# The second matrix of a channel MLP as seven products of quarters, with weights through DRAM and a new instruction order

## The chip, the core and the metric

The kernel runs on one core of one Trainium2 chip. The metric is the device time of one execution in microseconds; the median of several runs is what is compared. The engines are TensorE (PE in the profile; PEld is its weight load), VectorE (DVE), ScalarE (ACT), GpSimd (POOL) and SyncE (SP), which issues every DMA of this kernel.

## What is computed

Three blocks in a chain, on a batch of 4, a sequence of 576 and a width of 512, in float32:

```
# 1 block-causal attention, 8 heads of 64, blocks of 64 positions
scores = q @ k.T / 8, masked where block(i) < block(j);  x = softmax(scores) @ v
# 2 channel mixing with the token before
xk, xr = lerp(x, x_prev, mu_k), lerp(x, x_prev, mu_r)
x = sigmoid(xr @ w_r) * (relu(xk @ w_k)**2 @ w_v)          # 512->512, 512->1024->512
# 3 MLP mixer
u = x + (relu(x.T @ w_tok1) @ w_tok2).T                    # over tokens, 576->256->576
out = u + relu(u @ w_ch1) @ w_ch2                          # over channels, 512->1536->512
```

The change is about the last product, `relu(u @ w_ch1) @ w_ch2`: 2304 tokens, 1536 hidden channels, 512 outputs.

## The kernel before, in words

**Precision.** TensorE takes float32 operands in a rounded form (`F32R`). To keep accuracy every operand is split into a high part (the rounded value) and a low part (the rest), and each product is three matmuls: high by high, high by low, low by high (`mm3`, line 941; `mm_high` and `mm_low`, lines 928 and 933, for channel mixing). The splitting is work for the other engines: a cast for the high part (`copy`, line 467, on ScalarE or VectorE) and a subtraction for the low part (`less`, line 470, on VectorE or GpSimd). Weights come in as 64-bit floats and are first joined into one word (`split_chunk`, lines 485 to 522: steps `load`, `top`, `join`, `high`, `low`).

**Stages.** Attention (`attention`, `unit`, `pv`): for each batch element, each pair of heads and each block of 128 queries, scores (line 670), a mask (a memset of PSUM, line 698), the largest value (line 704), exponentials (line 723), the normalised probabilities as two float16 parts (lines 474, 476 and 750), a DMA transpose (line 756) and the product with v (line 835). Channel mixing (`channel_mix`): lerp and split (`mix`: steps `shifted`, `here`, `high`, `low`), then 240 matmuls of 256 or 320 columns for each part of a batch element; its result goes to DRAM (`xd`, line 1040) and comes back as `x` (line 1061). Token mixing (`front`, four of them). Channel MLP (`back`, five token tiles: one of 256 columns, four of 512): `split` and `rest` make the operand, twelve `g_group` steps of 12 matmuls make the hidden layer in PSUM (banks `b`), `g_high` (line 1178, ScalarE) and `g_low` (line 1181, VectorE) write its two parts, sixteen `y_group` steps of 9 matmuls make the four output blocks, `y_out` (line 1193) adds `u`, and `store` (line 1196) writes the result. The two parts of `w_ch2` are converted into SBUF once, in `c2a` (after channel mixing ends) and `c2b` (after the fronts end), and stay there.

**Order.** Every piece of work is a step with an engine, dependences and buffers (`Plan.step`). `Plan.schedule` plays all steps through with a table of costs (`c_pe`, `c_v`, `c_a`, `c_g`, `LAND` for a DMA's landing, a shared port for GpSimd and some VectorE steps) and emits the instructions of all engines in the order in which this play starts them; on each engine they then run in that order. Two long tables written into the file steer it: `RANK`, the priority of each of the 3464 steps (a permutation), and `ON`, the engine of each step that may run on more than one. `FILL` lets the plan put small matmuls of no use (line 538) into TensorE's planned gaps between two times of the plan.

Of the kernel before, what the change touches and what calls it, by code (L numbers as in the profile page):

```python
# [31 lines left out]
N2 = 3 * NC1 // 4  # L32
# [8 lines left out]
          "shifted", "square", "one"}  # L41

FILL = (4.0, 90.0)
FIFO = ("xh", "xl", "l", "o", "xt0", "xt1", "qkh", "uh")
CS, CV = 410, 256
LX, LPE, LSE, LAND = 0.15, 0.2, 0.12, 2.31
# [4 lines left out]
    xt0=4, xt1=4, mt=4, xh=8, xl=8, r=4, bxh=2, bxl=2, h1h=2, h1l=2, uh=4,  # L51
)

RANK = [int(x) for x in """
# [192 lines left out]
def c_v(n, psum=False):  # L247
    return 0.067 + n / 960 + 0.06 * psum


def c_v2(n):
    return 0.067 + n / 1920


def c_a(n, psum=False, ap=False):
    return (0.053 if psum else 0.093) + n / 1200 + 0.09 * ap
# [26 lines left out]
class Plan:  # L283
# [58 lines left out]
    def schedule(self):  # L342
# [21 lines left out]
        while done < len(self.steps):  # L364
# [39 lines left out]
            if s.shared:  # L404
                t = max(t, port)
                port = t + cost
# [1085 lines left out]
```

## Time and profile before

| | us |
|---|---|
| median of 3 runs (lowest, highest) | 792.9 (792.04, 796.18) |
| the profiled execution's own time | 793.54 |
| span of its profile | 791.8 |
| busy in the span: PE, PEld | 770.0, 673.3 |
| busy in the span: DVE, ACT, POOL | 499.9, 374.3, 116.7 |

The busy time of an engine is the union of its instructions' spans. A matmul's end is modelled and includes the way through the array, so a busy TensorE says that something was in flight, not that matmuls followed at the full rate; the rate is read from the distance of starts.

### The profile page before, as it was taken

What the parts mean: (1) busy time and instruction counts of PE and PEld (TensorE: products, weight loads), DVE (VectorE), ACT (ScalarE), POOL (GpSimd) and SP (SyncE); (2) the same over time, 40 slices, a digit from 0 to 9 for tenths busy, and PEclk for the clock granted to TensorE, in tenths of its full rate; (3) what the DMA queues carried; (4) which work ended last, traced back from release to release, by engine and by line L of the source; (5) the groups of instructions that cost most, each with busy time, mean ns of one, the idle gap of its engine ahead of it and who ended that gap; (6) DMA issues with size and microseconds to landing.
All of it is one profiled execution on the core that took longest, in us unless ns stands there. A gap on an engine that the chain in (4) does not pass through costs nothing.

```text
span 791.8 us, 16348 instructions
## 1 busy us (share of the span) xinstructions
PE 770.0 (97%) x6315; PEld 673.3 (85%) x6315; DVE 499.9 (63%) x1311; ACT 374.3 (47%) x1010; POOL 116.7 (15%) x143
## 2 busy tenths in 40 slices
PE   7899999998999999999999999999999999999998
PEld 5678898888988899999999988988888888888886
DVE  8999999978999899887836889622112121302111
ACT  6999877678687576745433344212102111300110
POOL 1222231231022121423203112200000000000000
PEclk9999999999999999999999999999999999999999
DMA  8789974967757857566123664100010000001001
GB/s 289 266 201 191 176 159 96 182 117 128 164 106 141 174 123 142 89 135 230 41 79 107 192 231 144 53 28 1 0 41 1 13 27 15 14 1 54 0 1 53
DMA packets 130671, 83.26 MB, mean 105 GB/s; under 512 B 104353, under 2 KB 112161, under 8 KB 130081
## 3 DMA queue, kind: packets, MB, share of 16 engines
q1 hardware_dynamic: 130592, 82.22, 43.5%
q8 instruction: 49, 0.80, 0.4%
q14 instruction: 30, 0.24, 0.1%
HBM read 48.11 MB, written 9.44 MB: 73 GB/s over the span
## 4 chain that ended last, share of the span: by engine, by line
PE 67%; DVE 9%; DMA 4%; ACT 2%; issue 1%; ACTq 0%; DVEq 0%; SPq 0%
PE b L941 38%; PE l L928 11%; PE l L933 6%; PE b L1090 4%; PE b L1111 3%; DMA pt<-pin 3%; DVE pin L750 2%; PE s L670 2%; PE o L835 2%; DVE nm L704 1%; PE b L1066 1%; DVE mt L906 1%; ACT p L723 1%; DVE xl L470 0%; DVE r L1035 0%
## 5 line engine op out<-in xcount | busy, mean ns | idle before, releaser
L941 PE MATMUL b<-uh,wx 128*128 128x512 f32 (+1 forms) x480 | 142.5, 373 | 0.0
L1178 ACT ACTIVATE wy<-b 128x512 fp32r<-128x512 f32 (+1 forms) x60 | 33.0, 555 | 219.3 <-PE b L941 219.1
L928 PE MATMUL l<-xh,wx 128*128 128x256 f32 (+1 forms) x768 | 124.4, 302 | 1.8 <-DVE r L1035 1.5
L928 PEld LDWEIGHTS l<-xh,wx 128*128 128x128 f32 x768 | 108.4, 190 | 8.5 <-DVE r L1035 1.7
L941 PE MATMUL b<-wy,c2a 128*128 128x512 f32 (+1 forms) x460 | 111.3, 368 | 0.0
L941 PEld LDWEIGHTS b<-uh,wx 128*128 128x128 f32 x480 | 87.6, 189 | 17.4 <-issue 0.5
L941 PEld LDWEIGHTS b<-wy,c2a 128*128 128x128 f32 x460 | 79.5, 189 | 15.3
L928 PE MATMUL l<-kh,wy 128*128 128x256 f32 (+1 forms) x512 | 76.6, 299 | 0.3 <-DVE r L1035 0.2
L941 PE MATMUL b<-gx,wx 128*128 128x512 f32 x192 | 75.4, 393 | 0.0
L928 PEld LDWEIGHTS l<-kh,wy 128*128 128x128 f32 x512 | 70.3, 189 | 3.2 <-issue 1.2
L723 ACT ACTIVATE p<-s,nb 128x384 f32<-128x384 f32 (+4 forms) x120 | 67.4, 564 | 11.3 <-DVE nb L476 5.2
L1193 DVE TENSOR_TENSOR x<-b,x 128x256 f32<-128x256 f32 (+7 forms) x32 | 13.5, 455 | 93.5 <-PE b L941 93.5
L750 DVE SCALAR_TENSOR_TENSOR pin<-p,rs,pin 128x384 f16<-128x384 f32 (+3 forms) x104 | 67.4, 657 | 5.0 <-ACT pin L474 4.5
L933 PE MATMUL l<-xl,wx 128*128 128x320 f32 (+1 forms) x384 | 67.0, 300 | 0.0
L1181 DVE SCALAR_TENSOR_TENSOR gx<-b,wy 128x512 fp32r<-128x512 f32 x32 | 21.8, 690 | 67.7 <-ACT wy L1178 67.7
L704 DVE TENSOR_REDUCE nm<-s 128x2 f32<-128x256 f32 (+4 forms) x80 | 63.2, 796 | 0.7 <-PE s L670 0.2
L933 PEld LDWEIGHTS l<-xl,wx 128*128 128x128 f32 x384 | 56.4, 190 | 0.5
L474 ACT ACTIVATE pin<-p,rs 128x512 f16<-128x512 f32 (+3 forms) x78 | 48.9, 638 | 15.2 <-DVE rs L742 6.8
L835 PEld LDWEIGHTS <-vb 128*64 128x64 f16 x1824 | 45.2, 111 | 12.6 <-issue 10.1
L835 PE MATMUL o<-pt,vb 128*64 128x128 f16 (+1 forms) x1824 | 50.6, 212 | 5.3 <-DMA pt<-pin 5.2
L1181 DVE SCALAR_TENSOR_TENSOR wy<-b,wy 128x512 fp32r<-128x512 f32 (+1 forms) x28 | 16.1, 576 | 48.8 <-ACT wy L1178 48.7
L941 PEld LDWEIGHTS b<-gx,wx 128*128 128x128 f32 x192 | 36.1, 188 | 8.3
(146 smaller groups left out, 1389.3 us busy)
## 6 DMA issues: line engine op xcount, KB each, us to landing
wst<-in_w_c SPq DMA_DIRECT2D x24, 256.0 KB, 3.0
qkf<-in_kq SPq DMA_DIRECT2D x12, 480.0 KB, 4.7
v<-in_v SPq DMA_DIRECT2D x16, 320.0 KB, 3.4
x<-xd SPq DMA_DIRECT2D x4, 1152.0 KB, 8.1
wst<-in_w_c2a SPq DMA_DIRECT2D x18, 256.0 KB, 2.8
qkl<-in_w_v SPq DMA_DIRECT2D x16, 256.0 KB, 3.2
stage<-in_w_k SPq DMA_DIRECT2D x9, 410.0 KB, 4.4
qkf<-in_kq SPq DMA_DIRECT2D x12, 256.0 KB, 3.3
```

What stands on the lines that cost most here:

```text
L474: self.nc.scalar.activation(out=out, in_=x, func=AF.Copy, scale=by)
L704: nc.vector.tensor_reduce(out=c["nm"][:, :nh], in_=m, axis=AX.XY if j == 4 else AX.X, op=ALU.max, negate=True)
L723: nc.scalar.activation(out=c[x], in_=s, func=AF.Exp, scale=0.125, bias=c["nb"][:, x:x + 1], accum_out=c["sm"][:, x:x + 1],)
L750: nc.vector.scalar_tensor_tensor(out=like(pin[:, w:w + n]), in0=c[x], scalar=rs, in1=like(pin[:, :n]), op0=ALU.mult, op1=ALU.subtract)
L835: nc.tensor.matmul(o[hh * D:hh * D + D, q0:q0 + rows], v[:, i, y, hh, :], st["pt", hh, j][:, x * (j + 1) + i, :], start=i == x == y == 0, ...
L928: self.nc.tensor.matmul(ps, ww[:, k, :], x[0][k], start=k == 0 and n == 0, stop=False)
L933: self.nc.tensor.matmul(ps, w[0][:, k, :], x[1][k], start=False, stop=k == kt - 1)
L941: self.nc.tensor.matmul(ps, ww[k], xx[k], start=k == 0 and n == 0, stop=k == kt - 1 and n == 2)
L1090: nc.tensor.matmul(ps, ww[:k, i, m * P:(m + 1) * P], xx[:k], start=i == 0 and n == 0, stop=i == NJ - 1 and ww is self.w1[1],)
L1111: nc.tensor.matmul(ps[:, :HT], c[hh, m][:, i * P:(i + 1) * P], ww[:, m, sl], start=n == 0, stop=n == 5)
L1178: nc.scalar.activation(out=gh(m), in_=d["g", m][:, :n], func=AF.Relu)
L1181: nc.vector.scalar_tensor_tensor(out=gl(m), in0=d["g", m][:, :n], scalar=0.0, in1=raw(gh(m)), op0=ALU.max, op1=ALU.subtract)
```

## The change

The hidden layer's values `B` (1536 by 512 tokens of a tile) and the weights `A` (`w_ch2`) are cut into quarters: 768 hidden channels by 256 outputs of the weights, 768 hidden channels by 256 tokens of the hidden layer. In place of eight products of quarters the kernel makes seven, of sums and differences of quarters (Strassen's form, Winograd's order of sums):

- `load_c2` replaces `c2a` and `c2b`. Twelve times it loads two chunks of `w_ch2` (the same `load`, `top`, `join`, `high`, `low` as before), makes four sums of 128x128 blocks (`term`), splits them (`high`, `low` of 512 columns), and stores 1 MB to a new DRAM buffer `wd` (8 matrices of 12 KB per partition). It may start when attention is over, and must be done before the second half of the memory is laid out (`to_back`).
- `back`: `g_out` writes the hidden layer once, unsplit, in float32 (ScalarE or VectorE), in place of `g_high` and `g_low`. `operand` splits a quarter in three steps of `high` and three of `low`, 512 columns each; `term` makes a difference of quarters in three steps of 512 columns. A tile of 512 tokens has 7 operands and 4 terms. Four operand buffers are shared by all tiles (`op`).
- `product` fetches one matrix of `wd` (128 rows of 12 KB, 1.57 MB) into one of three buffers (`rg`) and issues 36 matmuls of 256 columns (line for line the pattern of `mm3`). `add`, `keep` and `join` bring the seven results to `u`, by 256 tokens and two output blocks at a time. A tile of 512 tokens has 252 matmuls of 256 columns in place of 144 of 512. The tile of 256 tokens has no Strassen form: four products, 144 matmuls of 256 columns as before.
- TensorE's other work is unchanged. `mask` may now run on ScalarE too (an activation that writes -8e9), memsets of the start may run on GpSimd, one early activation (`word`) loads the exponential's table, `FILL` reaches to 320 instead of 90, all buffer kinds but seven are now handed out in order of rank (`FIFO`), and the plan's costs differ a little.
- `RANK` and `ON` are new, for 3791 steps. Counted over the two `ON` tables, steps that are in both kernels changed engine as follows (V VectorE, A ScalarE, G GpSimd; the count before, then after):

```
attention: mask V 64->27, A 0->37;  bias V 39->25, A 41->55;  first part of p V 36->28, A 92->100;  low of q,k V 15->11, G 9->13
weights of stage 2: low V 24->15, G 7->16;  high V 12->10, A 19->21;  top V 4->10, A 27->21
mixing: shifted V 23->13, A 41->51;  high V 22->13, A 42->51;  low V 36->24, G 28->40
        hidden high V 27->22, A 37->42;  hidden low V 38->34, G 26->30;  square V 11->17, A 34->36, G 19->11
new in load_c2: term V 26, G 22;  high V 5, A 7;  low V 7, G 5 (of 512 columns)
new in back: g_out V 27, A 33;  operand high V 52, A 49 and low V 47, G 54;  term V 27, G 21;  add, join, keep V 52, G 11, A 3
```

The diff, cut to its core (both tables left out):

```diff
-N2 = 3 * NC1 // 4
+NH, HC = NC1 // 2, NC // 2
...
-FILL = (4.0, 90.0)
-FIFO = ("xh", "xl", "l", "o", "xt0", "xt1", "qkh", "uh")
+FILL = (4.0, 320.0)
-LX, LPE, LSE, LAND = 0.15, 0.2, 0.12, 2.31
+LX, LPE, LSE, LAND, LTURN, LAP = 0.15, 0.2, 0.12, 1.4, 0.9, 0.15
...
+FIFO = frozenset(BUFS) - {"v32", "vm", "vd", "ve", "vs", "tw", "wst"}
...
-            step("V", 0.14, mask, r=[ts], w=[ts])
+            step("any", both(0.2, 0.14), mask, r=[ts, "none"], w=[ts])
...
+    def operand(self, src, toks, gate):
+        o = Buf("op")
+        for i in range(3):
+            def high(e, i=i):
+                self.copy(e, self.ops[o.slot][:, 0, 2 * i:2 * i + 2], src(i))
+            def low(e, i=i):
+                t = self.ops[o.slot]
+                self.less(e, t[:, 1, 2 * i:2 * i + 2], src(i), raw(t[:, 0, 2 * i:2 * i + 2]))
+            self.step("any", both(c_a(NC), c_v2(NC)), high, r=toks(i) + gate, w=[(o, (i, 0))])
+            self.step("any", both(v=c_v(NC), g=c_g(NC)), low, r=toks(i) + [(o, (i, 0))], w=[(o, (i, 1))])
+        return o
+    def product(self, w, o, x, begin=True, end=True, turn=False):
+        r = Buf("rg")
+        def fetch():
+            self.nc.sync.dma_start(raw(self.rg[r.slot]), self.wd[:, w])
+        def product(fs, ks, first, last):
+            ps, a, t = self.xb[x.slot], self.rg[r.slot].rearrange("p (k f h m) -> p k f h m", k=NH, f=2, h=2), self.ops[o.slot]
+            n = 0
+            for k in ks:
+                for f in fs:
+                    for y, z in ((0, 0), (0, 1), (1, 0)):
+                        n += 1
+                        self.nc.tensor.matmul(
+                            ps[:, f * HC:(f + 1) * HC], a[:, k, f, y], t[:, z, k],
+                            start=first and n == 1, stop=last and n == 6 * len(ks) * len(fs) // 2,
+                        )
+        self.step("S", 0.55, fetch, r=["wd", "sw3"], w=[r], dma=NH * 4 * P / 704)
...
-        def g_high(m):
-            nc.scalar.activation(out=gh(m), in_=d["g", m][:, :n], func=AF.Relu)
-        def g_low(m):
-            nc.vector.scalar_tensor_tensor(
-                out=gl(m), in0=d["g", m][:, :n], scalar=0.0, in1=raw(gh(m)), op0=ALU.max, op1=ALU.subtract
-            )
-        def y_group(i, k0, k1):
-            if k0 == 0:
-                d["y", i] = self.ps_b.tile([P, 512], F32, tag="b", name="b")
-            g = [[f(m) for m in range(NC1)] for f in (gh, gl)]
-            self.mm3(d["y", i][:, :n], self.c2[i], g, NC1, k0, k1)
+        def g_out(m, e):
+            g = self.g[:, m // NH, m % NH, :n]
+            if e == "A":
+                nc.scalar.activation(out=g, in_=d["g", m][:, :n], func=AF.Relu)
+            else:
+                nc.vector.tensor_scalar(out=g, in0=d["g", m][:, :n], scalar1=0.0, scalar2=None, op0=ALU.max)
...
+        o_b11 = self.operand(b11, k11, gate)
+        self.term(sub, tx, b12, b11, two(k12, k11), kx)
+        o_t1 = self.operand(tx, kx, gate)
+        o_b21 = self.operand(b21, k21, gate)
+        o_b22 = self.operand(b22, k22, gate)
+        self.term(sub, tx, b22, tx, two(k22, kx), kx)
+        o_t2 = self.operand(tx, kx, gate)
+        self.term(sub, b22, b22, b12, two(k22, k12), k22)
+        o_t3 = self.operand(b22, k22, gate)
+        self.term(sub, b21, b21, tx, two(k21, kx), k21)
+        o_t4 = self.operand(b21, k21, gate)
+        self.product(0, o_b11, p[0])
+        keep(p[0], ts)
+        add(p[0], 0, 0)
+        self.product(4, o_t1, p[1])
+        add(p[1], 0, 1)
+        add(p[1], 1, 1)
+        self.product(1, o_b21, p[2])
+        add(p[2], 0, 0, final=True)
+        self.product(7, o_b22, p[3])
+        add(p[3], 0, 1)
+        self.product(5, o_t2, p[4])
+        join(p[4], ts)
+        add(ts, 0, 1, final=True)
+        self.product(6, o_t3, p[5])
+        join(p[5], ts)
+        add(ts, 1, 1, final=True)
+        add(ts, 1, 0)
+        self.product(3, o_t4, p[6], turn=c == 4)
+        add(p[6], 1, 0, parts=((0,), (1,)) if c == 4 else ((0, 1),), final=True)
+    def load_c2(self, stage):
...
-        conv("c2a", lambda: self.c2a, N2 * DM, DM, self.i["w_c2a"], ["sw2"])
-        conv("c2b", lambda: self.c2b, (NC1 - N2) * DM, DM, self.i["w_c2b"], ["sw3"])
+        self.load_c2(stage)
+        step("X", 0.001, to_back, w=["sw3"], after=fronts + convs)
```

By its ranks the new order ends attention behind step 2382 of 3791 (2378 of 3464 before). Ahead of that place stand 1448 of the 1920 channel-mixing matmuls (1444 before), 830 steps of VectorE (924), 712 of ScalarE (643) and 124 of GpSimd (96). The c2 steps stand between there and the last front. Seven hidden-layer groups of the first 512-token tile stand between the first fetches and the first product, and the products of a tile stand mixed with the hidden-layer groups of the next one or two tiles. Only the seven products of the last tile stand back to back, at the end; the first three of their fetches start before or with the last hidden-layer group, the other four each behind a product.

## Rows read from the trace of the kernel before

**Rows 1.** The page's first part: busy us of TensorE and VectorE.
```profile
PE 770.0 (97%) x6315; PEld 673.3 (85%) x6315; DVE 499.9 (63%) x1311; ACT 374.3 (47%) x1010; POOL 116.7 (15%) x143
```

**Rows 2.** Windows of four stages: busy us of each engine, clock, DMA share, GB/s.
```profile
core 0: us, PE busy (x) PEld busy (x) DVE busy (x) ACT busy (x) POOL busy (x), PEclk, DMA share, GB/s
0.00:100.00 100.00, 89.88 (x1010) 71.99 (x1011) 94.38 (x275) 87.99 (x259) 22.95 (x37) 1.00 0.89 224
100.00:360.00 260.00, 252.09 (x3008) 232.54 (x3007) 236.58 (x651) 186.74 (x529) 60.30 (x66) 0.99 0.69 134
360.00:502.00 142.00, 142.00 (x991) 133.59 (x990) 105.14 (x262) 58.80 (x140) 30.13 (x39) 1.00 0.45 144
502.00:792.00 290.00, 285.99 (x1312) 235.23 (x1310) 63.76 (x126) 40.81 (x82) 3.27 (x4) 1.00 0.06 19
```

**Rows 3.** Chain that ended last, in order of time: start, us, what.
```profile
502.45 285.55 PE b L941 x1308
```

**Rows 4.** Timeline of TensorE, end of the 256-token tile's products: start, us.
```profile
503.72 8.80 PE L941 MATMUL b<-wy,c2a 128*128 128x256 f32 x72
512.36 0.40 PE L941 MATMUL b<-uh,wx 128*128 128x512 f32 x1
```

**Rows 5.** Last pieces of the chain at the end of the span.
```profile
788.02 0.69 DVE x L1193
```

**Rows 6.** Groups by shape, evictions of the last stage: count, busy, mean ns.
```profile
L1178 ACT ACTIVATE wy<-b 128x512 fp32r<-128x512 f32 x48 | 28.4, 598 | 209.8 <-PE b L941 209.6
L1193 DVE TENSOR_TENSOR x<-b,x 128x512 f32<-128x512 f32 x4 | 2.8, 692 | 15.4 <-PE b L941 15.4
L1193 DVE TENSOR_TENSOR x<-b,x 128x256 f32<-128x256 f32 x4 | 1.7, 425 | 10.9 <-PE b L941 10.9
```

**Rows 7.** Groups by shape, splitting steps of 512 columns on three engines.
```profile
L467 DVE CAST qkh<-qkf 128x512 fp32r<-128x512 f32 x5 | 2.1, 421 | 0.1
L467 ACT CAST qkh<-qkf 128x512 fp32r<-128x512 f32 x7 | 4.3, 615 | 1.3 <-DMA qkf<-in_kq 1.3
L470 DVE TENSOR_TENSOR qkl<-qkf,qkh 128x512 fp32r<-128x512 f32 x8 | 5.5, 683 | 0.0
L470 POOL TENSOR_TENSOR qkl<-qkf,qkh 128x512 fp32r<-128x512 f32 x4 | 5.8, 1438 | 10.6 <-DVE nb L476 6.2 <-ACT qkh L467 4.4
```

**Rows 8.** Groups by shape, steps that change engine in attention and mixing.
```profile
L698 DVE MEMSET s<- 64x128 f32 x64 | 10.5, 165 | 5.0 <-PE s L670 3.8
L711 ACT ACTIVATE nb<-nm 128x2 f32<-128x2 f32 x33 | 6.8, 205 | 13.1 <-DVE nm L704 13.1
L470 DVE TENSOR_TENSOR xl<-mt,xh 128x256 fp32r<-128x256 f32 x15 | 7.2, 483 | 0.0
L470 DVE TENSOR_TENSOR wx<-wst,wx 128x256 fp32r<-128x256 f32 x16 | 6.7, 419 | 0.1
L470 POOL TENSOR_TENSOR xl<-mt,xh 128x256 fp32r<-128x256 f32 x17 | 13.9, 825 | 55.5 <-ACT xh L467 29.7 <-DVE wx L470 10.8 <-DVE xh L467 8.4
L476 DVE TENSOR_SCALAR mt<-xt,omu 128x256 f32<-128x256 f32 x11 | 4.1, 387 | 0.0
```

**Rows 9.** Who TensorE waited for: us in total, times, longest.
```profile
PE o L835 <- DMA pt<-pin: 5.2, 6, 1.4
PE s L670 <- ACT p L723: 4.2, 8, 1.8
PE s L670 <- DMA qk<-in_kq: 4.1, 1, 4.1
```

**Rows 10.** Two windows: TensorE's clock in one, DMA share and GB/s in the other.
```profile
165.00:170.00 5.00, 5.00 (x33) 5.00 (x32) 2.77 (x8) 3.86 (x14) 2.86 (x4) 0.70 0.95 196
367.00:370.00 3.00, 3.00 (x27) 2.91 (x26) 2.46 (x6) 1.85 (x6) 1.62 (x2) 1.00 1.01 417
```

**Rows 11.** DMA issues: KB each, median us from issue to landing.
```profile
x<-xd SPq DMA_DIRECT2D x4, 1152.0 KB, 8.1
out<-x SPq DMA_DIRECT2D x4, 128.0 KB, 1.9
```

More of the change, by code (lines that the diff above doesn't have):

```diff
@@ L410, in schedule @@
                 ring = max(ring, end + s.lag) + s.dma
-                end = ring + LAND
+                end = ring + s.land
             s.end = end
@@ L1128, in front @@
             tp, th, tl = Buf("b"), Buf("bxh"), Buf("bxl") if rows == P else Buf()
-            add("PE", 0.109 * KD * rows / P, turn, i, rows, r=[tx, "ident"], w=[tp], after=last[:1])
+            add("PE", 0.109 * KD * rows / P, turn, i, rows, tp, r=[tx, "ident"], w=[tp], after=last[:1])
             t_ = steps[-1]
@@ new lines, in term @@
+    def term(self, op, out, a, b, toks, wtoks):
+        for i in range(3):
+            def term(e, i=i):
+                (self.nc.vector if e == "V" else self.nc.gpsimd).tensor_tensor(out=out(i), in0=a(i), in1=b(i), op=op)
+            self.step("any", both(v=c_v(NC), g=c_g(NC)), term, r=toks(i), w=wtoks(i))
+    def product(self, w, o, x, begin=True, end=True, turn=False):
[14 more added lines that the diff above has]
+        self.step("S", 0.55, fetch, r=["wd", "sw3"], w=[r], dma=NH * 4 * P / 704)
+        cuts = [((f,), range(NH)) for f in range(2)] if turn else [((0, 1), range(2 * i, 2 * i + 2)) for i in range(3)]
+        for z, (fs, ks) in enumerate(cuts):
+            m = 3 * len(fs) * len(ks)
+            toks = [(o, (k // 2, y)) for k in ks[::2] for y in range(2)]
+            self.step("PE", c_pe(m * HC, m), product, fs, ks, begin and z == 0, end and z == len(cuts) - 1,
+                      r=[r, "sw3"] + toks, w=[(x, f) for f in fs])
@@ L1226, in back @@
-        self.last_y = ys[-4:-3]
-        if c == 0:
-            step("X", 0.001, lambda: None, r=[], w=["hfree"])
-            z = self.plan.steps[-1]
-            for y in ys:
-                z.deps[y] = True
-                y.succ.append((z, True))
-                z.wait += 1
+            step("PE", c_pe(12 * n, 12), g_group, m, tp,
+                 r=tu + ["ul"] + (self.need("c1r", m) if m < KD else self.need("c1k", m - KD)), w=[tp])
+            step("any", both(c_a(n, True), c_v(n, True)), g_out, m, r=[tp, "sw2"],
+                 w=[("g", (m // NH, t, m % NH)) for t in range(nt)])
@@ new lines, in quarter, with part, add, y_out @@
+        def quarter(k, t):
+            return (lambda i: self.g[:, k, 2 * i:2 * i + 2, t * HC:(t + 1) * HC],
+                    lambda i: [("g", (k, t, 2 * i + y)) for y in range(2)])
+        def part(x, fs):
+            a = self.xb[x.slot] if x.tag == "x" else self.tp[x.slot]
+            return a.rearrange("p (a b) -> p a b", a=2)[:, fs[0]:fs[-1] + 1]
+        def add(x, fh, t, parts=((0, 1),), final=False):
+            for b, s, k, o in segs:
+                lo, hi = max(o, t * HC), min(o + k, (t + 1) * HC)
+                if lo >= hi:
+                    continue
+                s0, m = s + lo - o, hi - lo
+                for fs in parts:
+                    def y_out(e, fs=fs, b=b, s0=s0, m=m, at=lo - t * HC):
+                        u = self.u[b][:, 2 * fh + fs[0]:2 * fh + fs[-1] + 1, s0:s0 + m]
+                        (nc.vector if e == "V" else nc.gpsimd).tensor_tensor(
+                            out=u, in0=part(x, fs)[:, :, at:at + m], in1=u, op=ALU.add)
+                    def store(fs=fs, b=b, s0=s0, m=m):
+                        i0, i1 = 2 * fh + fs[0], 2 * fh + fs[-1] + 1
+                        nc.sync.dma_start(self.out[b, i0:i1, :, s0:s0 + m].rearrange("a p b -> p a b"), self.u[b][:, i0:i1, s0:s0 + m])
+                    toks = [(f"y{b}", (2 * fh + f, s0)) for f in fs]
+                    z = m * len(fs)
+                    step("any", both(v=c_v(z, x.tag == "x"), g=c_g(z) if x.tag != "x" else None), y_out, r=[(x, f) for f in fs], w=toks)
+                    if final:
+                        step("S", 0.55, store, r=toks, dma=z / 704)
@@ new lines, in keep, with join, sum_ @@
+        def keep(x, y):
+            def keep(e):
+                self.copy(e, part(y, (0, 1)), part(x, (0, 1)))
+            step("any", both(c_a(2 * HC, True), c_v(2 * HC, True)), keep, r=[x, "sw2"], w=[y])
+        def join(x, y):
+            def sum_():
+                nc.vector.tensor_tensor(out=part(y, (0, 1)), in0=part(x, (0, 1)), in1=part(y, (0, 1)), op=ALU.add)
+            step("V", c_v(2 * HC, True), sum_, r=[x], w=[y])
+        G = lambda k, t: quarter(k, t)
+        if nt == 1:
+            o1 = self.operand(*G(0, 0), ["sw2"])
+            o2 = self.operand(*G(1, 0), ["sw3"])
+            for fh in range(2):
+                p = Buf("x")
+                self.product(2 * fh, o1, p, end=False)
+                self.product(2 * fh + 1, o2, p, begin=False)
+                add(p, fh, 0, final=True)
+            return
@@ L1357, in to_mixer @@
                 p_.__exit__(None, None, None)
-            self.ps_b = open_pool("psb", bufs=6, space=PSUM, side="right")
+            psb = open_pool("psb", bufs=1, space=PSUM, side="right")
+            self.pb = [psb.tile([P, 512], F32, name=f"b{i}") for i in range(BUFS["b"])]
             self.right = open_pool("sb", bufs=1, side="right")
```

301 lines of the change are left out of this document (183 added, 118 removed), and 309 rows, old and new, of the table RANK.

## The prediction, written before the changed kernel was run

> **What bounds the kernel now.** I read the page's busy times first: TensorE has something in flight for 97% of the span [rows 1]. Then the four windows, which split that average [rows 2]. From 360 us on TensorE is never idle, while VectorE is busy for 74% and then 22% of the time; there only less TensorE work can save time. Before 360 us VectorE is the busiest after TensorE (94% in the first 100 us, 91% after), and ScalarE has 88% and 72%. TensorE's own numbers there hide slack: the 89.88 us of the first 100 hold useless fill matmuls, and what a modelled end covers does not count as idle. The chain in order of time ends in one unbroken piece of TensorE from 502.45 to 788.00 [rows 3], then one addition [rows 5]. The list of what TensorE waited for is short: 13.5 us in its three largest entries [rows 9], all before 360 us.
>
> **The price of a matmul.** In the trace 72 products of 256 columns run from 503.72 to 512.36 [rows 4], so 0.120 us each, with the same pattern of weights as the new products. The piece of rows 3 holds 1152 matmuls of 512 columns and 156 of 256 (144 products and the last 12 of the first tile's hidden layer): 285.55 - 156 x 0.120 = 266.8 us, over 1152 gives 0.2316. Half of that is 0.1158, so a narrow matmul costs 4% more for each column.
>
> **The change part by part.** The sum is made against the profiled execution's own 793.5 us (span 791.8 and 1.7 around it); the median of the runs shown is 0.6 lower.
>
> 1. *Seven products for eight.* Before, a tile of 512 tokens has 144 x 0.2316 = 33.35 us of TensorE, after it 252 x 0.120 = 30.24. Four tiles: 4 x 3.11 = -12.4 us, on the engine that sets the end. The 256-token tile has 144 narrow matmuls before and after: nothing. The Trainium skill, "TensorE: Matmul & The Clock Gate", section "Back-to-back issue gap", gives N/2.4 + 2.5 ns, an estimate of 109 and 216 ns for the two shapes. By it this part would be 4 x (144 x 0.2158 - 252 x 0.1092) = -14.2 us; the rows have both shapes and decide.
>
> 2. *The weights through DRAM.* Thirty-two fetches of 1.57 MB. With the queues full the DMA engines moved 417 GB/s [rows 10], so a fetch is 1.57/0.417 = 3.8 us of transfer and, with the 1.9 us of a small DMA [rows 11] for the way there and back, 5.7 us. A product takes 36 x 0.120 = 4.3 us. With three buffers a fetch starts when the product three places ahead has ended and has two products, 8.6 us, to land. So it is hidden, by 2.9 us, even in the last tile where the products stand back to back; in the other tiles hidden-layer groups of 2.8 us (12 x 0.2316) stand between. The slower row is the load of `x`, 1152 KB in 8.1 us, which shared its time with other loads [rows 11]: 1536 KB at that pace is 10.8 us, and the last four products would wait 2.2 us each, 9 us. I take 0, nearest to the row with full queues, and keep 9. The stores behind a fetch on SyncE's queue wait for additions that come right after a product, and the fetch behind such a store has the same 2.9 us.
>
> 3. *The operands.* On VectorE, ScalarE and GpSimd the last stage loses, in four tiles, `g_high` and `g_low` and gains 28 operands and 16 terms. By the counts of the engine table and 0.421, 0.615, 0.683 and 1.438 us for the split steps [rows 7] and about 0.6 for evictions [rows 6], VectorE rises from 67 to some 127 us, ScalarE from 46 to 60, GpSimd from 0 to 111, in a stage of some 280 us. That is under half of it each. The nearest row is the window from 360 to 502, where VectorE at 74% and GpSimd at 21% cost TensorE no idle time [rows 2]. So the cover is the TensorE queue itself: products of one tile stand among hidden-layer groups of the next. It is thin in the last tile only, where the chain from the last hidden group runs through the quarter `b21`, two differences and their splits. For seven products back to back I take half a microsecond of wait each, +3.5 us; the low end is 0, the high end the price of one GpSimd split, 1.438, at each of the 28 products of four tiles, +40.
>
> 4. *Weight conversion earlier and longer.* The c2 steps add 12 x (4 terms, a cast and a subtraction of 512 columns): VectorE +12, ScalarE +9, GpSimd +17 us, all with stores, to be done by the end of the fronts. The stage has VectorE at 105 of 142 us [rows 2]; 117 of 142 is 82%, below the 91% at which TensorE loses 3%. I take 0. If it were to cost what 91% costs, 142 x 3% = 4 us. The first fetch needs all twelve stores; seven hidden-layer groups (19 us) stand between the fetch and its product, so 5.7 us are covered.
>
> 5. *The new order and engines before 360 us.* Ahead of the last attention step VectorE has 94 steps less. Priced by shape (a mask 0.165, a lerp 0.387, a low part 0.483 of 256 columns [rows 8], the like for the others), the steps that left it are worth 27.6 us, ScalarE gains 20.1, GpSimd 27.4. VectorE's own instructions overlap by 0.067 us each (the prices of all 924 add up to 393 us, the windows show 331), so VectorE gets 27.6 - 94 x 0.067 = 21 us shorter. If VectorE alone set this stage, and stayed busy for the same 92%, attention would end 23 us earlier with the same matmuls behind it: that is the high end of the gain. The low end is 0: ScalarE goes from 275 of 360 us to some 290 of 340, 86%, and each step it takes over costs more there (0.205 against 0.165 for a small one). Between them: in the first 100 us ScalarE is as full as VectorE and gains nothing, so I take 2 there. From 100 to 360 TensorE's listed idle is 260 - 252.1 = 7.9 us, and from 165 to 170 us the granted clock is 0.70 in the mean, so partly at the lower of its two levels, 1.2 GHz in place of 2.4 [rows 10], a loss of 30% of 5 us, 1.5 us; the longer reach of `FILL` may give it back. I take 7 of these 9.4. Together -9.
>
> 6. *Small things.* The last addition is of 256 columns in place of 512: 0.692 - 0.425 [rows 6] = -0.3 us; the store behind it is 128 KB and lands in 1.9 us [rows 11]. The early table load is off the path, 0. A transpose that the new plan trusts to land earlier is a risk: 5.2 us were waited for transposes before [rows 9]; it stays in the range.
>
> Sum: 793.5 - 12.4 - 9 + 3.5 - 0.3 = 775.3 us for a profiled execution, less 0.6 for the median: **775 us**.
>
> **The rivals.**
>
> *A. The front gains nothing.* ScalarE and GpSimd take over what VectorE loses. For it: ScalarE's 88% in the first stage, and a low part that costs 0.483 on VectorE beside GpSimd's 0.825, but 0.419 in the weight steps [rows 8]. Against it: TensorE's waits name VectorE and ScalarE steps and transposes, which should shrink. Time: 775 + 9 = 784.
>
> *A2. GpSimd and VectorE take turns.* A subtraction of two SBUF tensors on VectorE and one on GpSimd would run one after the other. Then GpSimd's additional 27.4 us ahead of the attention's end come off VectorE's 27.6, and in the last stage 111 us of GpSimd and some 60 of VectorE add up to 170 of 280, still covered. Time as in A, 784, and up to 790 if the last tile's chain is stretched too. The 64 ns between 0.483 and 0.419 are all that the rows show for it, so little. The Trainium skill says in "SBUF — State Buffer", section "Who interferes with whom", that such a pair blocks fully; this trace agrees in direction only.
>
> *B. VectorE alone sets the front.* Its utilisation stays at 92%: the full 23 us come. Time: 775 - 14 = 761. For it: 94% and 91% in the windows. Against it: TensorE is in flight for 97% from 100 us on.
>
> *C. Products wait for operands: slower.* The place is the first matmul of each product, which needs low parts that GpSimd makes in 1.438 us, three in a row, and only four operand buffers let the split run ahead. At one such step late for each of 28 products it costs 40 us: 775 - 3.5 + 40 = 811. It becomes slower than before once the mean wait for each product passes 0.75 us ((793 - 772)/28). Against it: only some 45% of VectorE's and 40% of GpSimd's time is asked for.
>
> *D. Fetches too slow or the middle too full:* 9 us of part 2, or 4 of part 4 with half of A: 780 to 788.
>
> **How the numbers follow.** The measurement can tell about 0.5% (4 us) from no change. Main case, 769 to 781: 0.42. A and A2: 0.24 (784 to 790, a fifth of it within 4 us of before). B: 0.15 (757 to 768). D: 0.12 (a third of it within 4 us of before). C: 0.07. The likeliest is 775. The range for 8 in 10 leaves out half of B below and C with the worst of A2 above: 762 to 788. Faster than 789: 0.42 + 0.19 + 0.15 + 0.08 = 0.84. Within 4 us: 0.05 + 0.04 = 0.09. Slower: 0.07.
>
> **What would show it.** Right: matmuls `xb` from `rg` start 0.120 us apart; each fetch lands before the product ahead of it ends; TensorE has no idle time from the last transpose to the end but for under 4 us in the last tile; the last transpose-fed product of attention comes some 9 us earlier than before; VectorE's busy time ahead of it is some 20 us less; the clock stays at 1.0. Wrong: an idle TensorE whose releaser is GpSimd or VectorE at products (C), or a fetch (D); ScalarE near 95% up to attention's end, with that end where it was (A); narrow matmuls at more than 0.132 us, at which the seven products cost what the eight did (33.35/252).

## The result, and the profile after

The changed kernel takes 775.9 us in the median (773.99 to 776.17) beside 794.5 (792.04 to 796.3) of the kernel before: ratio 0.977, 95% interval 0.973 to 0.980. The profiled execution has a span of 774.3 us, against 791.8. The forecast was 775 of 762 to 788, so the number held; its two sides did not hold alike, and their errors cancel. The windows of the four stages (columns as in [rows 2]):

```profile
0.00:100.00 100.00, 89.53 (x959) 71.96 (x960) 91.04 (x243) 87.25 (x263) 40.56 (x52) 0.98 0.89 221
100.00:360.00 260.00, 255.57 (x3092) 237.91 (x3090) 226.32 (x590) 204.09 (x598) 76.52 (x82) 1.00 0.73 141
360.00:502.00 142.00, 141.97 (x973) 132.20 (x972) 124.80 (x300) 74.35 (x176) 50.27 (x63) 1.00 0.69 226
502.00:775.00 273.00, 267.62 (x1727) 244.41 (x1725) 142.01 (x206) 50.03 (x92) 109.20 (x80) 1.00 0.56 203
```

The reader is to see that the last stage got shorter with TensorE as full as before, while VectorE in it went from 63.76 us to 142 and GpSimd from 3.27 to 109. What TensorE waited for (us in total, times, longest), which answers to [rows 9]:

```profile
PE o L868 <- DMA pt<-pin: 4.0, 5, 1.1
PE s L700 <- DMA qk<-in_kq: 4.0, 1, 4.0
PE s L700 <- DVE tw L487: 2.0, 1, 2.0
PE s L700 <- ACT p L756: 1.6, 3, 1.1
PE l L961 <- ACT kt L1025: 1.4, 1, 1.4
PE x L1222 <- DVE x L1295: 1.0, 1, 1.0
```

Only the last of these lies behind attention, and no fetch (`rg` from `wd`) is among them. The chain in order of time (start, us, what) has the two kinds of matmul in pure pieces, first where the hidden layer stands alone and then from the last tiles:

```profile
511.38 21.79 PE b L974 x96
533.17 8.57 PE x L1222 x72
...
658.87 12.88 PE x L1222 x108
...
734.89 0.61 ACT g L1260
...
747.34 1.70 DVE op L490
749.03 1.44 DVE op L487
750.47 1.20 DVE op L490 x2
751.67 1.21 DVE x L1295 x2
752.88 0.04 issue
752.92 13.22 PE x L1222 x108
766.15 4.51 PE x L1222 x36
```

108 products in 12.88 us are 0.1193 each; 96 hidden-layer matmuls in 21.79 us are 0.2270, where the kernel before had 0.2316 over both layers [rows 3]. From 734.89 to 752.88 the chain runs mainly through operands on VectorE: this is the last tile. TensorE itself has work until 751.90 and then waits 1.0 us. What it waits for last is no operand (line 490 or 487) but two additions (line 1295). By the kernel they read the second product of the tile out of the PSUM bank that the fourth product needs, one of two such banks, and on VectorE they stand behind the operand steps, which end at 751.67.

The kernel splits well where attention ends, that is, at the first mixing matmul behind the last transpose-fed product. In the timeline of TensorE (start, us) this matmul is, first in the kernel before and then in the changed one:

```profile
359.32 1.22 PE L928 MATMUL l<-xh,wx 128*128 128x256 f32 x8
355.61 1.22 PE L961 MATMUL l<-xh,wx 128*128 128x256 f32 x8
```

So in these two executions attention gained 3.7 us and all behind it 17.5 - 3.7 = 13.8. The first of the two numbers is not firm: runs 3 and 7 below start the instructions of the changed kernel in the same order on every engine up to attention's end, and ended it at 353.27 and 352.01.

### The profile page after: what moved, and what is told of

It reads as the page before. It is cut to its first block, busy times and chain, and to the rows that moved or that the text cites. A ratio compares the mean times of both kernels' runs of the same rounds, so it can differ in the third digit from the quotient of the medians.

```text
span 774.3 us, 17660 instructions
## 1 busy us (share of the span) xinstructions
PE 754.7 (97%) x6745; PEld 686.5 (89%) x6745; DVE 584.2 (75%) x1336; ACT 415.7 (54%) x1128; POOL 276.6 (36%) x276
## 4 chain that ended last, share of the span: by engine, by line
PE 83%; DMA 8%; DVE 5%; ACT 2%; issue 1%; POOL 0%; SPq 0%; DVEq 0%; ACTq 0%
PE l L961 20%; PE b L974 19%; PE x L1222 16%; PE l L966 9%; DMA pt<-pin 6%; PE s L700 5%; PE o L868 4%; PE b L1123 4%; PE b L1144 3%; PE b L1099 1%; DMA v<-in_v 1%; DVE op L490 1%; DVE nm L737 1%; DMA stage<-in_w_k 1%; ACT pin L494 1%
## 5 line engine op out<-in xcount | busy, mean ns | idle before, releaser
L1222 PEld LDWEIGHTS x<-op,rg 128*128 128x128 f32 x1152 | 141.0, 190 | 3.5 <-DVE x L1295 1.2
L1222 PE MATMUL x<-op,rg 128*128 128x256 f32 x1152 | 141.9, 282 | 1.0 <-DVE x L1295 1.0
L974 PE MATMUL b<-ul,wx 128*128 128x512 f32 (+1 forms) x240 | 88.5, 369 | 0.0
L490 POOL TENSOR_TENSOR op<-g,op 128x512 fp32r<-128x512 f32 x35 | 50.1, 1440 | 106.2 <-DVE op L487 90.6
L487 ACT CAST op<-g 128x512 fp32r<-128x512 f32 x33 | 19.9, 620 | 93.5 <-PE x L1222 91.8
L737 DVE TENSOR_REDUCE nm<-s 128x2 f32<-128x1024 f32 (+4 forms) x80 | 63.9, 801 | 2.9 <-ACT s L729 2.6
L487 DVE CAST op<-g 128x512 fp32r<-128x512 f32 x33 | 21.2, 646 | 49.9 <-PE x L1222 49.8
L490 POOL TENSOR_TENSOR xl<-mt,xh 128x256 fp32r<-128x256 f32 (+1 forms) x40 | 35.3, 889 | 61.8 <-ACT xh L487 48.8
L490 POOL TENSOR_TENSOR kl<-kt,kh 128x256 fp32r<-128x256 f32 (+1 forms) x30 | 27.9, 933 | 81.3 <-ACT kh L487 56.3
L494 ACT ACTIVATE pin<-p,rs 128x384 f16<-128x384 f32 (+3 forms) x83 | 50.5, 623 | 7.9 <-DMA pt<-pin 5.9
```

Of the source, the lines that this page charges most:

```text
L487: (self.nc.scalar.copy if e == "A" else self.nc.vector.tensor_copy)(out, x)
L490: (self.nc.vector if e == "V" else self.nc.gpsimd).tensor_tensor(out=out, in0=a, in1=b, op=ALU.subtract)
L494: self.nc.scalar.activation(out=out, in_=x, func=AF.Copy, scale=by)
L737: nc.vector.tensor_reduce(out=c["nm"][:, :nh], in_=m, axis=AX.XY if j == 4 else AX.X, op=ALU.max, negate=True)
L974: self.nc.tensor.matmul(ps, ww[k], xx[k], start=k == 0 and n == 0, stop=k == kt - 1 and n == 2)
L1222: self.nc.tensor.matmul(ps[:, f * HC:(f + 1) * HC], a[:, k, f, y], t[:, z, k], start=first and n == 1, stop=last and n == 6 * len(ks) * le ...
```

## The experiments

Each time is a median, each ratio is to the kernel before on the same chip; "attention's end" is read as above from each run's timeline, so it is one execution.

**1. The old front with the new second layer.** The ranks and engines of all steps up to attention's end, and the planner's figures for them, are those of before (the core of the edit; both tables and the smaller costs are left out):

```diff
+OLD = [1]
+        if OLD:
+            self.land = 2.31
-                port = t + cost - LAP
+                port = t + cost - (0.0 if s.old else LAP)
```

> The changed kernel with the front part alone undone: every step up to the end of attention stands in the old order, on the old engines and with the old planner figures (VectorE's and the queue's sequences up to there are those of the kernel before); the second layer as seven products, its fetches and everything behind attention stay as changed. So the distance from the kernel before is the second layer's alone, and the distance from the changed kernel is the front's. Prediction on record: products -12.4 us, operand waits +3.5, so about 784 against 793, ratio 0.988 to 0.989. The theory formed on the trace after (front gained 3.7 us in all, the rest 13.8): ratio 0.982 to 0.984, about 779 to 780 against 793; attention ends 3 to 4 us later than in the changed kernel; after 360 us no difference from it. Rival (the front's gain comes from the new order carrying conversions out of the second half's way): the part behind attention gets slower than 419 us, ratio 0.99 or more.

Measured: 780.05 us, ratio 0.9835 (0.9811 to 0.986); behind attention's end lie 418.8 us, as in the changed kernel (418.7). So the second layer alone is worth 13.6 us, inside what the theory on the trace said and more than the 0.988 of the prediction's terms. The front is worth 4.1 by the two medians. Attention ends at 361.61, 6.0 us later than in the changed kernel and 2.3 later than in the kernel before, though VectorE, TensorE and the queue have the kernel before's order up to there: so much does one execution differ from another. Behind the other changed fronts (runs 2, 5, 6 and 9 to 12) it is 418.0 to 421.1 us, so this side hardly depends on the order of the front.

**2. Only the first 50 us in the old order.** In the changed kernel's start, the chain in order of time shows a load that is late:

```profile
16.69 7.21 DMA v<-in_v
...
24.66 0.41 DVE nm L737
```

The load of `v` takes 7.21 us to land, and VectorE, whose order is fixed, stands for 2.1 us before the step that needs it. TensorE's clock falls to 0.86 of full speed in the mean of the window from 20 to 30 us:

```profile
20.00:30.00 10.00, 8.01 (x65) 6.21 (x64) 7.89 (x24) 8.30 (x32) 3.64 (x5) 0.86 0.69 222
```

The edit puts the first 353 steps (by rank) back in the old order, on their old engines and with their old costs (tables and costs left out):

```diff
+CUT = 353
+        self.old = key < CUT
+        if self.old:
+            self.land = 2.31
```

> The changed kernel with only the steps of about the first 50 us back in the old order, on the old engines, with the old landing time of a load (2.31 instead of 1.4 us); the rest keeps its new ranks. Theory A (the new start trusts loads to land earlier than they do while the queues are full, VectorE stands before the landing of v, and some 5 us are lost there): the work of the first 50 us is done about 5 us earlier than in the changed kernel, and attention ends 3 to 5 us earlier, ratio 0.970 to 0.973 to the kernel before. Rival B (the loss is an investment: what the new start does early is missing later): the later stretch loses as much, ratio 0.975 to 0.980, as the changed kernel.

Measured: 778.71 us, ratio 0.9815 (0.979 to 0.9839), just outside what rival B said. The stall is gone,

```profile
20.00:30.00 10.00, 9.19 (x88) 7.08 (x86) 9.79 (x29) 9.86 (x36) 2.29 (x3) 1.00 0.91 300
```

and attention ends at 356.28, 0.7 us later than in the profiled execution with the stall. So theory A does not hold: the old start brings no gain. That the stall costs nothing does not follow, because other executions have no such stall: in runs 3 and 7, whose front has the changed kernel's order, the loads of `v` in the first 40 us landed within 6.1 and 5.6 us, and VectorE did not wait for one. The same window in run 3, and attention's end in both:

```profile
20.00:30.00 10.00, 9.65 (x90) 7.14 (x89) 9.89 (x32) 9.56 (x35) 4.23 (x6) 1.00 0.89 286
353.27 1.21 PE L961 MATMUL l<-xh,wx 128*128 128x256 f32 x8
352.01 1.22 PE L961 MATMUL l<-xh,wx 128*128 128x256 f32 x8
```

They end attention 2.3 and 3.6 us earlier than the execution with the stall. That the stall is all of this difference is not shown.

**3 and 4. The place of buffers.** The same instructions with the same widths took 0.2270 in one kernel and 0.2316 in the other. In both kernels some moving operands began 32 bytes off a multiple of 64:

```diff
             self.right = open_pool("sb", bufs=1, side="right")
+            self.right.tile([P, 8], F32, name="pad")
```

> The changed kernel with 32 bytes per partition laid in front of the right-hand buffers, nothing else: three of the four operand buffers, the three fetched weight buffers and the token mixer's weights, which began 32 bytes off a multiple of 64, now begin on one. Theory (a moving operand that begins off a multiple of 64 bytes costs TensorE some 1.5 ns in a 256-column and 4 to 5 ns in a 512-column matmul): products that read those three buffers go from 120 to about 118.5 ns apart (807 of 1152: -1.2 us), the token mixer's 104 full matmuls lose 4 ns each (-0.4 us): about 774.3 against 775.9, ratio 0.974 to 0.976. Rival (the place of a buffer does not matter): no change from the changed kernel's ratio of 0.977, and spacings as they were.

> The kernel before with the same 32 bytes in front of its right-hand buffers, nothing else: the hidden layer's low part and eight of its twelve low activations, which began 32 bytes off a multiple of 64, now begin on one. Theory: the first layer's matmuls of 512 columns go from 232 to about 227.5 ns, as in the changed kernel (576 of them, -2.6 us), the second layer's from 231.4 to 228 or less (576, -2 us), the token mixer's -0.4 us: 5 us less than the kernel before, ratio 0.993 to 0.995. So about 2.3 us of the change's gain would be a matter of where buffers begin, not of the products. Rival (the place does not matter): 232 ns stay, ratio 1.000.

Measured: after with the pad 773.77 us, ratio 0.9759 (0.9734 to 0.9784), not to be told from the changed kernel; its products start 0.120 apart (108 in 12.95 us) and its hidden layer stays where it was (96 matmuls in 21.77 us). Before with the pad 792.79, ratio 0.999 (0.9971 to 1.001); its unbroken piece of the last stage is shorter for the same 1308 matmuls, 283.53 against 285.55 [rows 3]:

```profile
502.44 283.53 PE b L941 x1308
```

The theory falls: the times do not follow the rule of 64 bytes, and the two profiles differ by 2.0 us in place of the 5 that it asked for. Whether the place of a buffer is the cause of these 2.0 us is not shown.

**5 and 6. Engines and order, each alone.** Run 5 keeps the new order and puts 401 steps ahead of attention's end back on their old engines (only `ON` differs). Run 6 keeps the new engines and takes the old order of all steps up to there, with the old planner figures (only `RANK` and the figures of run 1 differ).

> The changed kernel in its new order, but every step up to the end of attention on the engine that it had before (401 steps go back: masks and biases to VectorE, low parts from GpSimd to VectorE, and so on). Theory E (the front's gain is VectorE's relief, 14 us less of its work ahead of attention's end): VectorE's busy time ahead of 360 us goes back from 317 to about 330 us, attention ends about 4 us later than in the changed kernel, as in the old front: 780 us, ratio 0.982 to 0.985. Theory O (the gain is the order, which lets the second hundred microseconds run with TensorE almost without a gap whatever the engines): attention ends within 1.5 us of the changed kernel's, ratio 0.976 to 0.979. Later than the old front (ratio 0.987 or more): the order was made for these engines and is worth nothing without them.

> The other half: the old order of the steps up to the end of attention (with the old planner figures), on the new engines. Theory E: VectorE's relief alone brings the gain: attention ends as in the changed kernel, 776 us, ratio 0.976 to 0.979. Theory O: attention ends as with the old front or later, 780 us or more, ratio 0.982 or more. With both halves at about 780 or more, order and engines pay only together.

Measured: 801.97 us, ratio 1.0123 (1.0098 to 1.0148), and 805.36 us, 1.0153 (1.013 to 1.0177). Attention ends at 383.68 and 384.47, 24 to 25 us later than in the kernel before, which has neither, and 28 to 29 later than with both. Neither theory holds: each half alone is slower than the old whole. That order and engines pay only together is not shown by this, because a rival stands: the plan puts fill matmuls into the gaps that it foresees up to 320 us. In the changed kernel it placed 193, here (count, shortest, median and longest ns, first and last start) 393 and 499:

```profile
L560 PE MATMUL o<-ones x393: 243/246/368, 5.5 to 323.0; 128*128 128x192 bf16 x197
L568 PE MATMUL o<-ones x499: 242/246/368, 5.4 to 322.5; 128*128 128x192 bf16 x167
```

They keep TensorE busy for 40.2 and 49.8 us in place of 21.8, so up to 18 of the 28 and 28 of the 29 us can be theirs. No run was made without them.

**7. Two buffers for the fetched weights.**

```diff
-op=4, rg=3, wo=2
+op=4, rg=2, wo=2
```

> The changed kernel with two buffers for the fetched weight quarters in place of three: a fetch can be issued only when the product before the last has read its buffer, so that one product of 8.6 us is all that covers it. Theory (a fetch takes 6.4 us from issue to landing, 2.2 us less than a product): the products stay 0.120 us apart, waits of a product for its weights come to less than 2 us in all, ratio 0.976 to 0.979. Rival D (fetches are near the edge: the queue's issue, the stores of the result ahead of them and transfers under load eat the 2.2 us): 34 fetches late by 1 to 3 us, +30 to +100 us, ratio above 1.01.

(The 8.6 us in this expectation are two products, as part 2 of the prediction has it: one is 36 matmuls, 4.3 us. With that, a fetch of 6.4 us is 2.1 late.) Measured: 818.65 us, ratio 1.0324 (1.0292 to 1.0356), and attention's end is not later. Twelve fetches are waited for, 35.5 us in all (first row: total, times, longest). Then TensorE in the last tile, with the idle time and its releaser in brackets, and the windows around the first of these products:

```profile
PE x L1222 <- DMA rg<-wd: 35.5, 12, 6.7
724.46 4.42 PE L1222 MATMUL x<-op,rg 128*128 128x256 f32 x36
734.91 6.89 PE L1222 MATMUL x<-op,rg 128*128 128x256 f32 x36 [6.03 <-DMA rg<-wd]
748.53 6.91 PE L1222 MATMUL x<-op,rg 128*128 128x256 f32 x36 [6.73 <-DMA rg<-wd]
```

```profile
728.00:735.00 7.00, 0.97 (x9) 0.79 (x7) 2.92 (x5) 0.00 (x0) 1.26 (x1) 0.89 0.61 225
735.00:742.00 7.00, 6.80 (x36) 6.59 (x36) 0.17 (x1) 1.24 (x2) 2.12 (x2) 0.62 0.00 0
```

A late fetch is paid twice: 6 us without work, and then the granted clock is 0.62 in the mean, near the lower of its two levels, so that the product takes 6.89 us in place of 4.3. Rival D was one buffer away.

**8. Narrow matmuls in the kernel before.** The edit, shortened:

```diff
-self.mm3(d["y", i][:, :n], self.c2[i], g, NC1, k0, k1)
+for f in range(n // 256): matmul(d["y", i][:, f*256:(f+1)*256], w, x[:, f*256:(f+1)*256], ...)
```

> The kernel before, with the second layer's matmuls of 512 columns each cut into two of 256 with the same weights, nothing else: twice the matmuls, no product saved. Theory (a matmul of 256 columns takes 0.1195 us, one of 512 took 0.2314): four tiles of 288 x 0.1195 in place of 144 x 0.2314, 34.4 against 33.3 us, +4.4 us, ratio 1.004 to 1.007. Rival (narrow matmuls stay near a floor of issue, 0.132 us, where they follow one another without a new operand set): 38.0 a tile, +18.8 us, ratio 1.024.

Measured: 796.74 us, ratio 1.0038 (1.0019 to 1.0057): +3.2 us, the 4.4 of the theory lies inside the interval, the rival's 18.8 far outside. Its chain has both shapes:

```profile
529.68 24.96 PE b L941 x108
574.35 12.79 PE b L1194 x108
```

0.2311 and 0.1184. A narrow matmul takes half of a wide one here too, where two in a row have the same weights.

**9 and 10. What sets the front.** Run 9 leaves the 64 masks out, run 10 leaves out 224 low-part matmuls of the mixer's last product:

```diff
 def mask(e):
+    return                                             # 9
 def mm_low(self, ps, w, x, kt):
-    for k in range(kt):
+    for k in range(kt - 1 if kt == NF else 0, kt):     # 10
```

> The changed kernel without its 64 mask instructions (the causal mask of the diagonal tiles is left out, so the output isn't the reference's); the steps keep their places in the plan. It takes 27 x 0.164 = 4.4 us from VectorE and 37 x 0.266 = 9.9 us from ScalarE, all ahead of attention's end. Theory T (from 100 us on TensorE sets the front, 98% busy): attention ends within 1 us of the changed kernel's, ratio 0.975 to 0.978. Theory V (the two vector engines still set it): 4 to 8 us less, ratio 0.966 to 0.972.

> The changed kernel without seven of the eight low-part matmuls of each output tile of the channel mixer's last product (224 of 256 are left out, so the result is less exact); every other step keeps its place. 168 of them stand ahead of attention's end: 84 x 0.1465 + 84 x 0.120 = 22.4 us; the other 56 behind it: 7.5 us. Theory T: attention ends 20 to 22 us earlier, the kernel 27 to 30 us: 746 to 749, ratio 0.940 to 0.945. Theory V: the vector engines hold the front up, attention ends less than 8 us earlier, the kernel no more than 15: 761 or more, ratio 0.958 or more.

Measured: without masks 772.34 us, ratio 0.9731 (0.9692 to 0.977), attention's end at 354.85. This lies between the two theories' ratios, and the interval overlaps that of the changed kernel. Attention's end is 0.8 us earlier than in the changed kernel's profiled execution, as theory T asked, and later than in runs 3 and 7, so this run alone shows no gain of the front.

Without the matmuls 772.05 us, ratio 0.9724 (0.969 to 0.9759): 30 us of TensorE's work gone, 3.9 us between the medians. Attention ends at 349.54, 6.1 us earlier for 22.4 us less (2.5 and 3.7 earlier than in runs 7 and 3); behind it nothing was gained at all. The windows from 100 to 502 us, and TensorE's largest waits:

```profile
100.00:360.00 260.00, 243.88 (x2938) 222.71 (x2937) 228.32 (x599) 206.16 (x605) 78.93 (x84) 0.99 0.70 146
360.00:502.00 142.00, 135.55 (x888) 122.87 (x887) 119.48 (x285) 70.56 (x166) 48.01 (x60) 1.00 0.65 213
```

```profile
PE o L868 <- DMA pt<-pin: 11.2, 10, 2.1
PE s L700 <- ACT p L756: 6.5, 9, 2.5
PE l L961 <- DVE r L1068: 4.8, 5, 1.7
```

The waits for transposes, for ScalarE and for VectorE all grow as TensorE gets lighter. Between 370 and 440 us the chain of this run goes through the conversion of weights, of the second layer (`wo` and `ws`, the work of this change) and of the first (`wx`):

```profile
395.22 5.73 DMA wst<-in_w_c
...
405.57 1.53 DVE wo L487 x2
...
407.75 0.76 DVE ws L1437
...
411.47 1.47 POOL wx L490
...
412.95 3.32 DMA wst<-in_w_c
```

Theory T falls by run 10, though TensorE had 98% in this window of the changed kernel. Theory V is nearer there, but no single engine is shown to set the front: 14.3 us off the vector engines moved attention's end by no more than executions of the same order differ, 22.4 us off TensorE by 2.5 to 6.1.

**11 and 12. Two small parts of the front.** In run 11 the 37 masks of ScalarE go back to VectorE (`ON` alone). In run 12 one figure of the plan goes back:

```diff
-LX, LPE, LSE, LAND, LTURN, LAP = 0.15, 0.2, 0.12, 1.4, 0.9, 0.15
+LX, LPE, LSE, LAND, LTURN, LAP = 0.15, 0.2, 0.12, 2.31, 0.9, 0.15
```

> The changed kernel with the 37 masks that went to ScalarE back on VectorE (the plan lays its order around them anew). ScalarE gets 9.9 us back, VectorE takes 37 x 0.164 = 6.1 us more. Theory T: same time within 2 us, ratio 0.975 to 0.980. Theory V: VectorE's 6 us show, 780 to 782, ratio 0.982 to 0.986. Order theory (the ranks fit these engines and no others, as with the two halves that were tried apart): slower by more than the 6 us, ratio 0.987 or more.

> The changed kernel with one planner figure back: a load is taken to land 2.31 us after the queue is through with it, as before the change, in place of 1.4; ranks and engines as changed. Theory A, of the trace after (VectorE stands before the landing of v at 24 us because the plan trusts loads too early): the start loses 2 to 5 us less, 771 to 774, ratio 0.971 to 0.975. Rival B (what the start loses is made up by 80 us anyway, as the run with the old first 50 us showed; the figure only shifts the order of steps that were ranked with the other): no gain, ratio 0.976 to 0.99.

Measured: 787.05 us, ratio 0.9909 (0.9874 to 0.9944), and 783.74, ratio 0.9874 (0.9838 to 0.9909). Attention ends at 363.35 and 362.90. Moving 37 small instructions to another engine, or one figure of the plan, takes back all that the new front had gained, and more: the order theory and rival B. Here too the plan placed more fill matmuls, 292 and 226 for 193; those of run 11 keep TensorE busy for 8.8 us more, where its attention ends 7.7 us later, so they stand as a rival there. No run points to a better kernel: three lie 2 to 4 us below the changed one, two of them leave work out, and the third, with the pad, is within its interval.

## Why the prediction was right, point by point

**Seven products (-12.4).** Right, by its mechanism: 252 x 0.1193 = 30.06 us for a tile against 33.35, four times 3.29, -13.2. The old front with the new layer (run 1) shows the whole of this side alone, and run 8 the price of a narrow matmul. The 109 and 216 ns that the prediction worked out from the Trainium skill, "TensorE: Matmul & The Clock Gate", section "Back-to-back issue gap", come from a formula that the page gives for a matmul standing alone. The chain has 119.3 and 227 to 232, 10 to 16 ns above it.

**Not in the prediction: the hidden layer got faster.** 576 matmuls of 512 columns at 0.2270 in place of 0.2316, -2.6 us, in instructions that the diff leaves alone. That the place of their operands does it was argued from the fact that nothing else differs, and runs 3 and 4 refute the one rule that I tried; the cause stays open.

**Fetches (0).** Right, no wait for one. A fetch took 6.4 us from issue to landing in the median, not 5.7, with 8.6 to land in, a margin of 2.2 instead of 2.9. Run 7 shows that the third buffer is all of it. The margin is thin: in runs 2, 5, 6 and 12, with three buffers, a product waited once for its fetch, 0.3 to 1.1 us.

**Operands (+3.5).** Right place, smaller size, and another releaser: one wait of 1.0 us, in the last tile, at the end of the chain that the prediction named. What it ended with was the two additions that free a product's PSUM bank; the operand steps cost time only because these additions stand behind them on VectorE. The same wait of 1.0 us is in every run with the new layer and three fetch buffers. Rival C needed 0.75 us at each of 28 products.

**Conversion in the middle (0).** Right: TensorE is busy for 141.97 of 142 us. By the chain of run 10 little was left over: with less TensorE work there, it goes through the conversion.

**The front (-9).** This is the term that was mis-sized. It gained 3.7 us in the two profiled executions and 4.1 by the medians of run 1. Over all profiled executions of either order (old: 359.32, 361.61, 359.53 and 362.09 us in the kernel before and runs 1, 4 and 8; new: 355.61, 353.27 and 352.01 in the changed kernel and runs 3 and 7) the means are 7.0 apart. So the gain lies between 4 and 7, and single executions are 3 us apart on either side.

For the first 100 us the prediction said -2. At 100 us the kernel before had started 104 score matmuls and 384 transpose-fed ones, runs 3 and 7 had started 104 and 101 of the one, 384 of the other and 9 and 6 more of the mixing (windows by line): by these counts about 1 us or less gained. The profiled execution of the changed kernel, with the late load, had 98 and 344, which at the rates of the rest of that stage is about 2 us of work less.

From 100 us to attention's end the prediction said -7. There the profiled execution did that work as well and still came out 3.7 us ahead, so close to 6, and run 3, 6.0 ahead in all, close to 5. This half is nearer; how it comes about is open. The longer reach of `FILL`, which the prediction named for part of it, was not used: the last fill matmul starts at 48.4 us. The working took most of TensorE's listed idle, 7.9 us, as what could be had, and VectorE's relief of 21 us as what would bring it. Run 10 shows what is doubtful in that: of 22.4 us less TensorE work only 2.5 to 6.1 arrive, so the listed idle is not the slack; its waits for transposes, ScalarE and VectorE all grow. And VectorE got only 14.4 us shorter up to attention's end (316.0 against 330.4), because its instructions got longer: a `join` of 410 columns (line 526, before 506) 763 ns in place of 580, 13 of them; an output of 128 columns to `pin` (line 783, before 750) 423 in place of 357, 24 of them. GpSimd is busier beside them, 115 us for 83, but that it is the cause in this stage is not shown.

**Sum.** Ahead of attention's end -3.7 for -9; behind it -13.8 for -9.2 (products 0.8 better, the hidden layer 2.6, operands 2.5 better, 1.3 of other differences the other way). Two errors of 5 us cancelled in this pair of executions; that the total met 775 so closely is luck.

**Rivals.** A2 was real in the last stage. Its groups by shape in the changed kernel (count, busy, mean ns):

```profile
L490 DVE TENSOR_TENSOR op<-g,op 128x512 fp32r<-128x512 f32 x29 | 26.2, 918 | 0.1
L487 DVE CAST op<-g 128x512 fp32r<-128x512 f32 x32 | 20.7, 650 | 49.9 <-PE x L1222 49.8
L1204 DVE TENSOR_TENSOR tx<-g,tx 128x512 f32<-128x512 f32 x8 | 9.5, 1216 | 0.7 <-ACT g L1260 0.7
```

A low part that VectorE made in 683 ns takes 918, a cast 650 in place of 421 [rows 7], a difference 1216. The timeline shows that this hangs on GpSimd: two low parts of the same shape on VectorE, the first while GpSimd stood idle for 4.37 us, the second beside its subtractions:

```profile
743.67 0.68 DVE L490 TENSOR_TENSOR op<-g,op 128x512 fp32r<-128x512 f32 x1
747.25 1.78 DVE L490 TENSOR_TENSOR op<-g,op 128x512 fp32r<-128x512 f32 x1
746.89 3.30 POOL L490 TENSOR_TENSOR op<-g,op 128x512 fp32r<-128x512 f32 x2 [4.37 <-ACT op L487]
```

Counted over the stage, VectorE's low parts take 0.68 us where GpSimd is idle (21 of them) and 1.15 in the mean, up to 1.78, where they stand mostly beside it (17). GpSimd's take 1.29 with VectorE idle (10) and 1.47 otherwise (38); the 1438 of before [rows 7] had VectorE busy beside it. VectorE was put at 127 us for this stage and has 142, and the hidden-layer groups cover it, as the rival said for this place. The Trainium skill, "SBUF — State Buffer", section "Who interferes with whom", says that a VectorE instruction with two SBUF inputs contends with a GpSimd instruction that reads SBUF, and that the order of issue decides who blocks. The rows agree on the pair; both engines lose here, VectorE more. B did not come: VectorE had 89% of the time up to attention's end, not 92%, and taking TensorE work away moved that end too.

## What to carry to other kernels

A transfer is hidden by the buffers ahead of it, so count them in units of what one of them covers: here 2 x 4.3 us covered 6.4 and 4.3 did not, and the difference was some 43 us. Where several engines are each 82% to 96% busy (ScalarE, VectorE and TensorE up to attention's end), the idle time listed for the fullest says little about what can be won; taking work from one engine and looking at what arrives at the end does. One profile of each kernel is too little for a gain of a few us: the same order ended attention up to 3.6 us apart. An order written out by hand belongs to its engines and its figures: every part of it that was taken alone here ended attention later than the whole, though in part this may be the fill matmuls that the plan added.

## What the runs showed of the hardware beyond that

- In the last stage VectorE's subtractions of 512 columns took 0.68 us with GpSimd idle and up to 1.78 beside it, its casts 0.42 alone (25) and 1.06 in the mean beside it (17); GpSimd's subtractions took 1.29 alone and 1.47 beside VectorE.
- After 6 us without a matmul, 36 products took 6.89 us in place of 4.3, at a granted clock of 0.62 in the mean; in the changed kernel, without such gaps, it stays at 1.00 from 100 us on.
- A load of 320 KB that landed in 7.2 us in one execution was not over 6.1 and 5.6 in two others with the same order of the queue.
- The same 512-column matmuls on the same weights stood 0.2270 us apart in one kernel and 0.2311 to 0.2316 in the others.
